# Batch 0's k loaded in two halves, and a GpSimd wait for the second half placed behind the issue of w3's load

## The chip, the cores and the metric

The kernel runs on one core of one Trainium2 chip. The metric is device time in microseconds (us). Three runs of the kernel before took 166.56, 165.96 and 166.01 us; the median is 166.01 us.

The engines are named as the profile names them: PE (TensorE, matrix multiply), PEld (its weight loads), DVE (VectorE), ACT (ScalarE), POOL (GpSimd) and SP (SyncE). Loads and stores run on 16 DMA engines; the queue that issues a load is POOL's (software queue) or SP's (hardware queue).

## The reference, cut to what matters

```python
# q, k, v: (8, 8, 576, 64); phi: (8, 8, 576, 32); w1, w2, w3: (512, 768); w_out: (768, 512)
a = exp(phi - max(phi, axis=2)); a = a / sum(a, axis=2)
k_m = einsum('bhsm,bhsd->bhmd', a, k)
v_m = einsum('bhsm,bhsd->bhmd', a, v)
attn = softmax(q @ k_m.T / 8)          # over the 32 memory slots
x = (attn @ v_m) reshaped to (4608, 512)
h = maximum(maximum(x @ w1, x @ w2), x @ w3)
out = h @ w_out                        # (4608, 512), float32
```

## The kernel before

The kernel holds one batch of the attention at a time, as 4 pairs of heads (`NP`) on 128 partitions. The inputs are float32 in memory; q, k, v and the weights become bfloat16 while they are loaded, which is done by loads issued from GpSimd. phi stays float32; batch 0's phi is loaded in two halves on SP's queue.

No scheduler orders the work. `tc.manual_schedule()` is in force, and the long string in lines 594 to 617 is the program: each word names a step, its index and its batch, and `issue` (L561) emits the instructions of that step on their engines in just this order. Each engine's queue runs in order, so the place of a word fixes its place in every queue that it touches.

The steps that matter here, all of batch 0 unless said otherwise:

- `L1` (`load_kv`, L95) loads all of k, `L3` (`load_q`, L107) all of q, `H1` and `H3` the first and the second half of v by pairs of heads. `H0` and `H2` would do the same for k; the code has them, and the order before doesn't use them.
- `Y2`, `Y3`, `Y0`, `Y1` load w3, w_out, w1 and w2 (L114 and L122).
- `E` (L225) is the exponential of phi on ACT. `B0` (L238) multiplies it with k, and with a column of ones for the sums; its loops run over 9 chunks outside and the 4 pairs of heads inside, so the fifth of its 72 matmuls already reads the second half of k. `N0` and `K0` scale and transpose the result. `I` makes the identity that the transposes use.
- `Q0`, `Q1` (L306) transpose q on DVE, `S` (L320) makes the scores, `M` and `R` the softmax denominators, `X` the normalised attention.
- `W0` to `W2` (L178) transpose w3 on PE, `O0` to `O3` (L189) multiply it with w_out. `D` (L424) folds the weights with v's product: `D0` and `D1` need w1 (and w2), `D2` w2. `F` (L456) is the first layer's matmul and maximum, `T` (L488) the second layer with its output rows.
- `Z` (L155) are matmuls on a tile of zeros, whose result nobody reads.

Of the loads on GpSimd's queue the order is: k, q, (the identity and two small memsets), w3, w_out, v in two halves, w1, w2, then for batch 1 phi, k, q and v, then for batch 2 v, k, phi and q, and so on. The loads share eight completion semaphores in turn, so each issue from the ninth load on waits until the load issued eight before it has landed. Before a buffer is written again, an issue also waits for the engines that still read it.

Of the kernel before, what the change touches and what calls it, by code (L numbers as in the profile page):

```python
# [9 lines left out]
BF16 = mybir.dt.bfloat16  # L10
# [5 lines left out]
def kernel(  # L16
# [12 lines left out]
    nc = tc.nc  # L29

    B, H, S, D = q.shape
    M = phi.shape[-1]
    P = 128
    NP = H // 2
# [10 lines left out]
    const = ctx.enter_context(tc.tile_pool(name="const", bufs=1))  # L45
# [30 lines left out]
    loaded = {}  # L76
# [8 lines left out]
    def load_ph(b):  # L85
        ph = inp.tile([P, NP, NC, M], FP32, name="ph")
        loaded.setdefault(b, {})["ph"] = ph
        dst = ph.rearrange("p j c m -> p j (c m)")
        if b == 0:
            for h in halves:  # L90
                nc.sync.dma_start(out=dst[:, h], in_=by_pair(phi, b)[:, h])
        else:
            nc.gpsimd.dma_start(out=dst, in_=by_pair(phi, b))

    def load_kv(b, i, h=slice(0, NP)):  # L95
        kv = loaded.setdefault(b, {})["kv"] = kvos[b % 2]
        nc.gpsimd.dma_start(  # L97
            out=kv[:, 1 - i, h].rearrange("p j c d -> p j (c d)"),
            in_=by_pair((k, v)[i], b)[:, h],
        )  # L100

    def pack(b, i):
        nc.gpsimd.tensor_copy(  # L103
            out=kvrs[b % 2][:, :, :, D * i : D * (i + 1)], in_=kvos[b % 2][:, 1 - i]
        )

    def load_q(b):  # L107
        qq = inp.tile([P, NP, NC, D], BF16, name="qq")
        loaded.setdefault(b, {})["q"] = qq
        nc.gpsimd.dma_start(  # L110
            out=qq.rearrange("p j c d -> p j (c d)"), in_=by_pair(q, b)
        )

    def load_w(i):  # L114
        w = (moe_w1, moe_w2, moe_w3)[i]
        nc.gpsimd.dma_start(
            out=w_sb[:, :, i], in_=w.rearrange("(j p) f -> p j f", p=P)
        )
# [2 lines left out]

    def load_wo():  # L122
        nc.gpsimd.dma_start(out=wo_sb, in_=moe_w_out.rearrange("(t p) c -> p t c", p=P))  # L123

    load_ph(0)

# [21 lines left out]
    def one_bank():  # L148
        return psum[:, int(next(banks))]
# [5 lines left out]
    def warm_up(n):  # L155

        po = one_bank()
        for _ in range(n):
            nc.tensor.matmul(  # L159
                po[:, 0:BANK], lhsT=warm[:, 0:P], rhs=warm, start=True, stop=True  # L160
            )
# [46 lines left out]
    def w_diff(n):  # L208

        c, end = n * BANK, (n + 1) * BANK  # L210
        while c < end:
            e = min(end, (c // DF + 1) * DF)
            nc.vector.tensor_tensor(
                out=w12[:, :, c:e],
                in0=w12[:, :, c:e],
                in1=w_sb[:, :, 2, c % DF : c % DF + e - c],
                op=ALU.subtract,
            )
            c = e
# [5 lines left out]
    def att_exp(b, js=slice(0, NP)):  # L225
        s = st.setdefault(b, {})
        if "e" not in s:
            s["e"] = work.tile([P, NP, NC, M], BF16, name="e")
        nc.scalar.activation(out=s["e"][:, js], in_=loaded[b]["ph"][:, js], func=AF.Exp)  # L229
# [8 lines left out]
    def att_kv(b, part=None):  # L238
        s = st[b]
        kvp = two_banks()  # L240
        s["kvp", part] = kvp
        kv = loaded[b]["kv"]
        nd = {None: 2 * D + 1, 0: 2 * D, 1: D}[part]
        kvr = kvrs[b % 2]
        for c in range(NC):
            for j in range(NP):
                for a in range(NG):
                    r = slice(HP * a, HP * (a + 1))
                    nc.tensor.matmul(  # L249
                        kvp[M * j : M * (j + 1), a, 0:nd],  # L250
                        lhsT=s["e"][r, j, c, :],
                        rhs={
                            None: lambda: kvr[r, j, c, 0:nd],
                            0: lambda: k_and_ones(kv, r, j, c),
                            1: lambda: kv[r, 0, j, c, :],
                        }[part](),
                        start=(c == 0),
                        stop=(c == NC - 1),
                        tile_position=(HP * a, M * j),
                    )  # L260
# [141 lines left out]
    def att_rec(b, g):  # L402
        s = st[b]
        nc.vector.reciprocal(out=s["sm", g], in_=s["sm", g])  # L404
# [156 lines left out]
    def issue(b, n, swap):  # L561

        i = int(n[1:]) if len(n) > 1 else None
        {
            "I": lambda: [make_identity(nc, ident)]
            + [nc.gpsimd.memset(x[:, :, :, 2 * D : 2 * D + 1], 1.0) for x in kvrs],
            "Y": lambda: load_w(i) if i < 3 else load_wo(),
            "L": lambda: load_ph(b) if i == 0 else load_q(b) if i == 3 else load_kv(b, i - 1),
            "H": lambda: load_kv(b, i % 2, halves[i // 2]),
            "r": lambda: pack(b, i),  # L570
            "E": lambda: [att_exp(b, h) for h in (halves if b == 0 else [slice(0, NP)])],
            "B": lambda: att_kv(b, i),
            "N": lambda: att_kv_norm(b, i),
            "K": lambda: att_kv_t(b, swap, i),
            "Q": lambda: att_q(b, i),
            "S": lambda: att_score(b),
            "a": lambda: att_t(b, i),
            "s": lambda: att_sum(b, i),
            "c": lambda: att_rec(b, i),
            "m": lambda: att_mul(b, i),  # L580
            "X": lambda: (ones_mul if (b, i) in ONES else att_back)(b, i),
            "M": lambda: ones_sum(b, i),
            "R": lambda: ones_rec(b, i),
            "D": lambda: fold(b, i, swap),
            "F": lambda: ffn1(b, i, swap),
            "T": lambda: ffn2(b, i, swap),
            "W": lambda: w3_t(i, swap),
            "O": lambda: w3_o(i, swap),
            "V": lambda: w_diff(i),
            "Z": lambda: warm_up(i),  # L590
        }[n[0]]()


    for w in """
        E@0 L1@0 L3@0 Z25@0 B0@0 I@0 N0@0 Z2@0 K0@0! Q0@0 Q1@0 Z9@0 S@0 Z2@0 M0@0 M1@0
        R0@0 Y2@0 R1@0 W0@0 Y3@0 W1@0 W2@0 Z6@0 O1@0 H3@0 O3@0 O2@0 H1@0 X1@0 B1@0 X0@0 N1@0
        K1@0 O0@0 Y0@0 D1@0! D0@0! D3@0 F8@0 F10@0 F2@0 V0@0 F6@0 F0@0! Y1@0 D2@0 D4@0 F4@0
        L0@1 V1@0 F1@0 E@1 F3@0 L1@1 F5@0 F9@0 F7@0 L3@1 F11@0 B0@1 T3@0 N0@1 K0@1! L2@1 Q1@1
        L2@2 L1@2 Q0@1 L0@2 V2@0 T0@0! L3@2 S@1 T1@0 a0@1 s0@1 c0@1 m0@1 B1@1 N1@1 a1@1 L1@3
        K1@1 s1@1 D0@1 D1@1! D2@1 c1@1 m1@1 X0@1 L3@3 r1@2 X1@1 T2@0! L2@3 F6@1 F10@1 F7@1 F2@1  # L600
        F3@1 F4@1 F0@1 r0@2 E@2 F5@1 F1@1 F11@1 L0@3 L0@4 F8@1 L2@4 F9@1 B@2 D3@1 N@2 Q1@2
        T0@1! K@2 T2@1! r0@3 Q0@2 S@2 a0@2 a1@2 s1@2 c1@2 m1@2 T4@1! D1@2! s0@2 D2@2 c0@2 m0@2
        X1@2 D0@2 T3@1 Q0@3 L3@4 X0@2 Q1@3 T1@1 F0@2 F4@2 F8@2 F6@2 F9@2 E@3 F7@2 r1@3 F5@2
        F10@2 F1@2 B@3 L1@4 D3@2 N@3 L0@5 F2@2 F11@2 E@4 F3@2 L1@5 K@3 r1@4 L2@5 T2@2! S@3 T3@2
        a0@3 s0@3 c0@3 m0@3 D0@3 D2@3 a1@3 s1@3 c1@3 X0@3 D1@3! Q0@4 m1@3 T1@2 L3@5 L2@6 T0@2!
        X1@3 F10@3 r0@4 F2@3 F4@3 E@5 Q1@4 r0@5 F5@3 F3@3 L1@6 F8@3 B@4 N@4 D3@3 F9@3 F6@3
        F11@3 L0@6 K@4 F0@3 F7@3 F1@3 S@4 a0@4 T4@3! s0@4 a1@4 D0@4 c0@4 s1@4 r1@5 c1@4 D3@4
        m0@4 X0@4 Q0@5 T0@3! D1@4! D2@4 B@5 T3@3 m1@4 X1@4 L0@7 F10@4 Q1@5 N@5 F8@4 K@5 F6@4
        F9@4 S@5 F7@4 L3@6 F2@4 F4@4 a0@5 L1@7 a1@5 F0@4 s0@5 r1@6 F3@4 D0@5 r0@6 s1@5 c1@5 E@6
        D3@5 m1@5 c0@5 F1@4 T1@3 L2@7 F11@4 L3@7 E@7 F5@4 m0@5 B@6 D1@5! D2@5 X1@5 N@6 T2@3!  # L610
        X0@5 F6@5 F8@5 Q0@6 Q1@6 K@6 F4@5 F9@5 S@6 F7@5 r0@7 a0@6 F2@5 a1@6 s0@6 c0@6 F0@5
        F10@5 m0@6 F1@5 s1@6 c1@6 F11@5 F5@5 T0@4! F3@5 X0@6 T2@4! r1@7 D0@6 D1@6! Q0@7 B@7
        m1@6 N@7 X1@6 T2@5! K@7 T3@4 Q1@7 S@7 a0@7 F2@6 s0@7 a1@7 s1@7 c1@7 m1@7 c0@7 F4@6
        T4@5! D3@6 D2@7 D0@7! T0@5! D3@7 D2@6 X1@7 m0@7 D1@7! T1@4 X0@7 F6@7 F3@6 T1@5 F4@7
        F8@7 F0@7 F5@6 F10@6 F7@7 F9@7 F10@7 F5@7 F0@6 F11@7 F6@6 F1@7 F7@6 F2@7 F8@6 F11@6
        F9@6 F1@6 F3@7 T0@6! T0@7! T3@5 T2@7! T2@6! T1@6 T1@7 T3@6 T4@7! T3@7
    """.split():
        n, b = w.rstrip("!").split("@")
        issue(int(b), n, w.endswith("!"))
# [30 lines left out]
```

## Time and profile before

| | |
|---|---|
| median of 3 runs | 166.01 us |
| span of the profiled execution, first to last instruction | 163.9 us |
| outside the span, against the median | 2.1 us |
| PE busy | 153.8 us (94%) |
| ACT, DVE, POOL busy | 100.5, 90.4, 68.8 us |
| bytes moved by DMA | 31.77 MB, mean 194 GB/s |
| software queue's share of the 16 engines' time | 68.5% |
| granted TensorE clock, mean | 1.000 |

The page lists one profiled execution. A line of the timeline has a start and a duration in us, an engine, a line of the code, an operation, the tile it writes and the tile it reads, a count, and in square brackets how long the engine sat idle before it and what released it. In the chain of waits, a line is a start, a duration and what the chain ran through: where a DMA stands there, the time is from its issue to its landing. In a table of stages, a row is a stretch of time and gives, per engine, busy time and number of instructions, then the granted clock, the DMA engines' share and what they moved in GB/s. The bytes are counted as they are written, so a load from float32 to bfloat16 counts half of what is read.

The five largest shares of the chain by line are the matmuls of L497 (25%) and L466 (22%), the load of phi (14%), the load of the weights (12%) and the matmuls of L506 (7%).

### The profile page before, as it was taken

Reading aid. Unit: us, or ns where it says so; the run is one execution under the profiler, and the core shown is the slowest. Engines: PE = TensorE matmul, PEld = TensorE weight load, DVE = VectorE, ACT = ScalarE, POOL = GpSimd, SP = SyncE. Lnnn points to the kernel's source line nnn. Section 1 sums busy time; section 2 is a strip of 40 time slices with the busy share of each in tenths; the row PEclk is TensorE's granted clock in tenths of the full one; section 3 lists DMA queues with packets and bytes.
Section 4 is the critical chain, followed back from the end, with each engine's and each line's share of the span. In section 5 each row is a group of like instructions: output and inputs, shape, how many; then the busy total and the mean of one; then the engine's idle time right before and its main releaser. Section 6 shows DMA issues by size and latency. Waiting matters only on the chain.

```text
span 163.9 us, 4837 instructions
## 1 busy us (share of the span) xinstructions
PE 153.8 (94%) x2080; PEld 85.3 (52%) x2080; DVE 90.4 (55%) x181; ACT 100.5 (61%) x151; POOL 68.8 (42%) x70
## 2 busy tenths in 40 slices
PE   7958798999899999999999999999999999999990
PEld 2423544664376436753673565576553467744450
DVE  2013703898837765759399669879749228810000
ACT  4104535935496488778885989994658976323320
POOL 7911115100698276938929986755403200000000
PEclk9999999999999999999999999999999999999999
DMA  5999999999999999999999999996313230014333
GB/s 149 167 201 207 207 209 226 264 208 209 258 310 239 209 272 361 263 219 294 247 265 206 236 352 254 167 235 148 127 72 119 79 128 0 0 68 179 141 128 130
DMA packets 21958, 31.77 MB, mean 194 GB/s; under 512 B 1200, under 2 KB 16560, under 8 KB 21936
## 3 DMA queue, kind: packets, MB, share of 16 engines
q0 software_dynamic: 16064, 21.43, 68.5%
q1 hardware_dynamic: 5728, 9.90, 17.1%
q8 instruction: 16, 0.26, 0.6%
q10 hardware_dynamic: 144, 0.13, 0.2%
q14 instruction: 6, 0.05, 0.1%
HBM read 39.32 MB, written 9.44 MB: 297 GB/s over the span
## 4 chain that ended last, share of the span: by engine, by line
PE 66%; DMA 27%; POOL 3%; issue 1%; ACT 1%; ACTq 0%; POOLq 0%
PE psum L497 25%; PE psum L466 22%; DMA ph<-in_phi_dram 14%; DMA w_sb<-in_moe_w_dram 12%; PE psum L506 7%; PE psum L440 4%; PE psum L249 3%; PE psum L333 2%; PE psum L515 1%; POOL kvo L97 1%; PE psum L538 1%; ACT e L229 1%; PE psum L298 1%; POOL wo_sb L123 1%; POOL qq L110 0%
## 5 line engine op out<-in xcount | busy, mean ns | idle before, releaser
L497 PE MATMUL psum<-wo_sb,hT 128*128 128x512 bf16 x210 | 51.4, 380 | 0.2
L466 PE MATMUL psum<-attn,wp 128*128 128x288 bf16 x384 | 50.5, 286 | 0.1
L479 DVE TENSOR_TENSOR hT<-psum,h 128x576 bf16<-128x576 f32 x48 | 34.2, 749 | 18.2 <-PE psum L466 12.1
L466 PEld LDWEIGHTS <-wp 128*128 128x128 bf16 x384 | 36.7, 98 | 13.2 <-issue 2.0
L172 ACT COPY ot<-psum 128x512 f32<-128x512 f32 x35 | 20.7, 591 | 32.3 <-PE psum L506 25.2
L497 PEld LDWEIGHTS <-hT 128*128 128x128 bf16 x210 | 19.2, 98 | 24.2 <-issue 4.5
L103 POOL COPY kvr<-kvo 128x2304 bf16<-128x2304 bf16 x12 | 25.4, 2116 | 14.1 <-DMA kvo<-in_k_dram 6.4
L172 ACT CAST wp<-psum 128x1024 bf16<-128x1024 f32 (+1 forms) x31 | 29.3, 997 | 3.0 <-PE psum L440 2.1
L170 ACT ACTIVATE h<-psum 128x576 bf16<-128x576 f32 x47 | 28.4, 659 | 3.2 <-PE psum L466 3.1
L409 POOL TENSOR_TENSOR t<-t,sm 128x576 bf16<-128x576 bf16 x14 | 16.1, 1158 | 25.6 <-DVE sm L404 25.5
L506 PE MATMUL psum<-wp,attn 128*128 128x512 bf16 x62 | 18.4, 379 | 0.0
L159 PE MATMUL psum<-warm 128*128 128x512 bf16 x44 | 12.0, 424 | 1.2 <-DVE warm L128 1.2
L313 DVE STREAM_TRANSPOSE qT<-qq 128x576 f32<-128x576 f32 x16 | 11.7, 747 | 1.3 <-DMA qq<-in_q_dram 1.3
L342 ACT ACTIVATE e<-psum 128x576 bf16<-128x576 f32 x16 | 9.6, 652 | 3.7 <-PE psum L333 3.7
L229 ACT ACTIVATE e<-ph 128x1152 bf16<-128x1152 f32 (+1 forms) x9 | 9.6, 1065 | 2.9 <-DMA ph<-in_phi_dram 2.9
L395 DVE TENSOR_REDUCE sm<-t 128x18 f32<-128x576 bf16 x14 | 10.3, 738 | 0.2
L387 DVE STREAM_TRANSPOSE t<-e 128x288 f32<-128x288 f32 x14 | 6.4, 465 | 6.2 <-ACT e L342 6.0
L506 PEld LDWEIGHTS <-attn 128*128 128x128 bf16 x62 | 6.1, 98 | 7.1
L97 POOL DMA_DIRECT2D kvo<-in_v_dram x9 | 6.7, 747 | 7.1 <-PE psum L249 4.1
L249 PEld LDWEIGHTS <-e 64*32 64x32 bf16 x720 | 6.9, 90 | 4.9 <-issue 3.6
L555 DVE COPY ot<-psum 128x256 f32<-128x256 f32 x1 | 0.4, 425 | 15.4 <-PE psum L546 15.4
L110 POOL DMA_DIRECT2D qq<-in_q_dram x8 | 6.2, 769 | 5.9 <-DMA w_sb<-in_moe_w_dram 5.9
(57 smaller groups left out, 113.8 us busy)
## 6 DMA issues: line engine op xcount, KB each, us to landing
out_dram<-ot SPq DMA_DIRECT2D x35, 256.0 KB, 5.6
kvo<-in_k_dram POOLq DMA_DIRECT2D x8, 576.0 KB, 13.3
qq<-in_q_dram POOLq DMA_DIRECT2D x8, 576.0 KB, 12.6
ph<-in_phi_dram POOLq DMA_DIRECT2D x7, 576.0 KB, 15.0
kvo<-in_v_dram POOLq DMA_DIRECT2D x7, 576.0 KB, 16.6
w_sb<-in_moe_w_dram POOLq DMA_DIRECT2D x3, 768.0 KB, 20.3
wo_sb<-in_moe_w_out_dram POOLq DMA_DIRECT2D x1, 768.0 KB, 15.9
ph<-in_phi_dram SPq DMA_DIRECT2D x2, 288.0 KB, 3.1
```

The source lines that it names most:

```text
L103: nc.gpsimd.tensor_copy(out=kvrs[b % 2][:, :, :, D * i : D * (i + 1)], in_=kvos[b % 2][:, 1 - i])
L159: nc.tensor.matmul(po[:, 0:BANK], lhsT=warm[:, 0:P], rhs=warm, start=True, stop=True)
L170: nc.scalar.activation(out=out_, in_=in_, func=AF.Relu)
L172: nc.scalar.copy(out=out_, in_=in_)
L229: nc.scalar.activation(out=s["e"][:, js], in_=loaded[b]["ph"][:, js], func=AF.Exp)
L249: nc.tensor.matmul(kvp[M * j : M * (j + 1), a, 0:nd], lhsT=s["e"][r, j, c, :], rhs={None: lambda: kvr[r, j, c, 0:nd], 0: lambda: k_and_one ...
L313: nc.vector.transpose(out=s["qT"][:, j].rearrange("p j c r e -> p (j c r e)").bitcast(FP32), in_=loaded[b]["q"][:, j].rearrange("p j c d - ...
L409: nc.gpsimd.tensor_tensor(out=t, in0=t, in1=s["sm", g].unsqueeze(2).to_broadcast([P, S // HP, R, 2]), op=ALU.mult,)
L466: nc.tensor.matmul(acc[:, h, 0:SH], lhsT=wps[b][:, g, w * DF + ft * P : w * DF + (ft + 1) * P], rhs=attn[:, g, c0 : c0 + SH], start=(g == ...
L479: nc.vector.tensor_tensor(out=hT[:, ft, (b % 2) * S : (b % 2 + 1) * S].rearrange("p (h n) -> p h n", h=2), in0=a, in1=s["h1", ft], op=ALU.max,
L497: nc.tensor.matmul(po, lhsT=hT[:, fc, c0 : c0 + P], rhs=wo_sb[:, fc, :], start=(n == 0), stop=False,)
L506: nc.tensor.matmul(po, lhsT=attn[:, g, c0 : c0 + P], rhs=wp3s[b][:, g, :], start=False, stop=(g == NG - 1),)
```

## The change

k of batch 0 is loaded by two loads of two pairs of heads each in place of one load of four (`H0 H2` for `L1`). A new step, `G0`, copies two elements of the second half of k (the last pair of heads, one partition) into a new tile `gate` on GpSimd; nobody reads that tile. The copy reads what the second load writes, so GpSimd waits there until it has landed. In the order `G0` stands behind `Y2` and ahead of `Y3`, so on GpSimd's queue it comes after the issue of w3's load and ahead of the issues of w_out, v, w1, w2 and everything behind them. The function has another form, for q, which isn't used.

```diff
+    gate = const.tile([1, 2], BF16, name="gate")
+
+    def wait_for(b, n):
+
+        x = loaded[b]["q"][0:1, 0, 0, 0:2] if n else loaded[b]["kv"][0:1, 1, NP - 1, 0, 0:2]
+        nc.gpsimd.tensor_copy(out=gate, in_=x)
...
+            "G": lambda: wait_for(b, i),
...
-        E@0 L1@0 L3@0 Z25@0 B0@0 I@0 N0@0 Z2@0 K0@0! Q0@0 Q1@0 Z9@0 S@0 Z2@0 M0@0 M1@0
-        R0@0 Y2@0 R1@0 W0@0 Y3@0 W1@0 W2@0 Z6@0 O1@0 H3@0 O3@0 O2@0 H1@0 X1@0 B1@0 X0@0 N1@0
+        E@0 H0@0 H2@0 L3@0 Z25@0 B0@0 I@0 N0@0 Z2@0 K0@0! Q0@0 Q1@0 Z9@0 S@0 Z2@0 M0@0 M1@0
+        R0@0 Y2@0 G0@0 R1@0 W0@0 Y3@0 W1@0 W2@0 Z6@0 O1@0 H3@0 O3@0 O2@0 H1@0 X1@0 B1@0 X0@0 N1@0
```

## The prediction

> **What bounds the kernel now.** I read the chain of waits first, to see what the end hangs on, then the two queues around the change.
>
> ```profile
> 6.53 20.26 DMA w_sb<-in_moe_w_dram
> 26.79 0.59 issue
> 27.39 23.77 DMA ph<-in_phi_dram
> 51.17 1.17 ACT e L229
> 52.39 0.81 PE psum L249 x70
> ```
>
> From 6.5 to 51.2 us the chain is two loads, each some 20 us from issue to landing; from there it is PE without a break. A load of 768 KB that takes 20 us was queued, not slow. The trace's packet records show the queue: packets of 1536 bytes (w3) begin at 9.96 us, as the first engines end q, and packets of 1024 bytes (w_out) at 13.9, as they end w3. Each of the 16 DMA engines works through the loads in the order of issue, without a pause.
>
> GpSimd's queue, timeline:
>
> ```profile
> 1.24 0.93 POOL L97 DMA_DIRECT2D kvo<-in_k_dram  x1 [0.80 <-POOLq L634]
> 2.17 0.75 POOL L110 DMA_DIRECT2D qq<-in_q_dram  x1
> ...
> 3.57 0.76 POOL L116 DMA_DIRECT2D w_sb<-in_moe_w_dram  x1
> 4.33 0.83 POOL L123 DMA_DIRECT2D wo_sb<-in_moe_w_out_dram  x1
> 5.14 1.42 POOL L97 DMA_DIRECT2D kvo<-in_v_dram  x2
> 6.53 1.53 POOL L116 DMA_DIRECT2D w_sb<-in_moe_w_dram  x2
> 10.09 0.76 POOL L93 DMA_DIRECT2D ph<-in_phi_dram  x1 [2.03 <-DMA kvo<-in_k_dram]
> ```
>
> Eight loads are issued by 8.06 us, long before the engines reach most of them; the next issue waits for k.
>
> PE's queue, timeline:
>
> ```profile
> 9.94 0.80 PE L249 MATMUL psum<-kvo,e 64*32 64x128 bf16 x72 [1.54 <-DMA kvo<-in_k_dram]
> ...
> 20.25 4.04 PE L192 MATMUL psum<-wo_sb,w3T 128*128 128x512 bf16 x18 [0.97 <-DMA wo_sb<-in_moe_w_out_dram]
> ...
> 30.65 0.30 PE L440 MATMUL psum<-w_sb,kvt 64*32 64x256 bf16 x8
> ```
>
> PE goes at the pace of the loads: it waits 1.54 us for k, 0.97 for w_out, and its weight load waits 0.2 for w2 at 30.65. A load counts as landed when the last of 16 engines has written its completion. By the records, 14 of k's 16 completions come between 6.88 and 8.01 us, median 7.50, and the last two at 8.72 and 9.53. These engines stay late: the last completion is at 12.37 for q, 16.12 for w3, 19.92 for w_out, 26.54 for w1 and 30.28 for w2, each time 1.5 us after the thirteenth. So PE and the 51 us of the load chain hang on one engine that fell behind before 9.6 us.
>
> The stages show when the engines are slow (last number: GB/s):
>
> ```profile
> 4.00:5.00 1.00, 1.00 (x4) 0.35 (x3) 0.00 (x0) 0.51 (x2) 1.00 (x2) 1.00 0.94 129
> 5.00:6.00 1.00, 1.00 (x6) 0.49 (x5) 0.00 (x0) 0.37 (x1) 1.00 (x3) 1.00 1.06 160
> 6.00:7.00 1.00, 1.00 (x7) 0.45 (x5) 0.00 (x0) 0.00 (x0) 1.00 (x2) 1.00 1.20 189
> 7.00:8.00 1.00, 1.00 (x6) 0.43 (x5) 0.00 (x0) 0.00 (x0) 1.00 (x2) 1.00 1.13 174
> 8.00:9.00 1.00, 0.40 (x2) 0.00 (x0) 0.00 (x0) 0.00 (x0) 0.06 (x1) 1.00 1.21 202
> 9.00:10.00 1.00, 0.06 (x9) 0.09 (x17) 0.00 (x0) 0.00 (x0) 0.00 (x0) 1.00 1.17 189
> 10.00:11.00 1.00, 1.00 (x74) 0.71 (x73) 0.17 (x2) 0.00 (x0) 0.76 (x1) 1.00 1.19 201
> 11.00:12.00 1.00, 0.61 (x5) 0.23 (x4) 0.61 (x2) 0.01 (x1) 0.00 (x0) 1.00 1.16 210
> ```
>
> The steady rate is 208 to 210. Short of 208 the stages lose 0.38, 0.23, 0.09, 0.16, 0.03, 0.09 and 0.03 us: 1.0 us for the mean engine, nothing later. The late engine loses its 1.0 plus the 2.0 by which 9.53 lies behind the median: about 3 times the mean. The poor stretch covers the burst of issues (1.24 to 8.06) plus about 2 us, and k's own first packet comes 2.3 us after its issue begins.
>
> **The split of k.** One more issue: v's two halves cost 1.42 us together, so 0.7 each. k's second half is issued by 2.9 us, q by 3.65, w3 by 5.1, each 0.7 later than now. A load is ready for the engines 1.34 us after its issue ends (k: 3.51 less 2.17). The second half is then ready at 4.2 with the first busy until about 5.5; q at 5.0, needed at 6.9; w3 at 6.4, needed at 10.0. All covered, by 1.3, 1.9 and 3.6 us; without cover each would cost its 0.7. The identity ends at about 4.2 and is used at 11.66. One more completion per engine costs 0.02 us (its record is 22 ns). PE can run 4 of 72 matmuls (0.04 us) before the second half: nothing.
>
> **The wait.** Behind it on GpSimd's queue stand w_out, v twice, w1, w2, batch 1's phi and k. An issue that waits for a load starts 0.56 us after it (10.09 against 9.53). The copy isn't in the trace: between 0.10 (memset of one column) and 2.12 us (copy of 2304 columns). I take 0.1, as it moves two elements. With k no earlier than now, w_out is issued from 10.2 to 11.0 and ready at 12.4; the first engine wants it at 13.9. Cover 1.5 us; a copy of 2.12 would overrun it by 0.5. Then v to 12.5, w1 and w2 to 14.0, phi to 14.8, k to 15.5. Their packets are wanted from 17.7 (v), 20.5 (w1) and 24.3 (w2) on. Batch 1's q waits for w3 to land (16.12), as now. From there the queue is the old one.
>
> **What it buys.** Issues stop between 5.1 and about 10 us while k and q transfer. If the slow packets follow the issues, the losses after 6 us (0.40 of 1.0 for the mean engine) go away there, times 3 for the late engine: 1.2 us. Bounds: nothing, if they do not follow the issues, and 1.8, if all from 5.1 on goes (0.61 times 3). The six issues then come as a burst at 10.2 to 14.8. The nearest row is the burst of three at 25.31 to 28.14: by the records its packets of 28 to 31 us ran over their usual time by 0.03 us per engine in all. Twice that, times 3, is 0.2 given back; the other bound is 1.2, the whole again. Sum: 1.2 less 0.2 less 0.02, so 1.0 us earlier at k, q, w3, w_out, w1, w2 and, at 51.17, batch 2's phi. PE follows one for one, since w3's transposes, w_out's product and the folds are each released by these landings. The span goes from 163.9 to 162.9; with the 2.1 us that the median has outside the span, 165.0 us.
>
> The Trainium skill speaks against this. "DMA: Bandwidth & Descriptors", section "Latency and other measured facts", says that two DMA engines, 7 and 15, usually lag, and guesses at the ports of the partitions that hold the software queue's descriptor rings, which all engines read. The trace agrees on two that lag most (8.72 and 9.53); it doesn't show their numbers. By reading alone, though, the lag would grow with every load, and the gain would be nothing: 166.0 us. Here it stands still after 10 us, from 12.37 against a median of 10.66 (q) to 26.54 against 24.82 (w1): 1.71 and 1.72.
>
> **Rivals.**
> *No net effect, 166.0 us (165.2 to 166.8).* The engines are slow because they start, whatever GpSimd does; or the lag leaves k and comes back on w_out. For it: the worst loss, 0.61 of 1.0, lies before 6 us, under issues that the change keeps, and single later issues (13.00, 16.71) cost no visible rate. Against it: slowness lasts to 10 us, with q's packets slow to 10.1 and those after it at their usual time.
> *Slower, 166.9 us: the burst collects the lag again, in the weights.* The start keeps 60% of the 2.0 us lag, 1.2; six back-to-back issues at the start's price (2.0 over 8, 0.25 each) add 1.5: 2.7, so 0.7 more than now, plus 0.2 for the mean rate. Place: between 12 and 17 us, on w3 and w_out. It decides when w_out's last completion comes after 19.92. For it: 6 issues follow without a gap, as at the start. Against it: the burst at 25 us cost a tenth of that per issue.
> *Slower: the issues come too late.* Read as drawn, the chain has 20.26 us from w1 and w2's issue to landing, and 6 us later issue would end at 172. Against it: the time is queueing. With the long copy it would be 0.5, so 166.5.
> *The change doesn't do what it says:* the wait holds nothing back that matters, as in the first rival.
>
> **How the numbers follow.** Forecast 0.46, no net effect 0.29, burst 0.21, late issues 0.04. Faster by over 0.5% (0.83 us, about what a measurement of this kernel can tell from no change) is the forecast's case: 0.46; same 0.29; slower 0.25. The forecast's own range is 164.2 to 165.2 (gain 1.8 down to 0.8). The whole, with the slower cases, is 164.2 to 167.1.
>
> **What would show it.** Right: k's last landing near 8.5 and PE's first matmul on it near 8.9; w_out's product near 19.2; the fold of w2 near 29.6; phi of batch 2 near 50.2; GB/s above 190 from 6 to 10 us and near 208 from 12 to 17. Wrong: k earlier but w_out's product still at 20.25 (the lag moved); a dip in GB/s at 12 to 17 (burst); a DMA share below 0.9 near 13 to 14 (starved); or PE, though released earlier, waiting for something else by 52 us.

## The result, and the profile after

| | before | after |
|---|---|---|
| median of 7 runs | 166.01 us (165.55 to 166.73) | 164.87 us (164.30 to 165.42) |
| ratio, with 95% interval | | 0.9925 (0.990 to 0.995) |
| span of the profiled execution | 163.9 us | 163.7 us |

The kernel became 0.75% faster, 1.14 us on the medians. The two profiled executions differ by only 0.2 us. The profiled execution of the changed kernel, the first of its series, was the slowest of seven: 165.42 us with a span of 163.7, where the other six had spans of 162.5 to 163.5. Which execution of the kernel before was profiled isn't on record, but of 35 later runs of it, with spans of 163.6 to 165.4, a span of 163.9 is among the shortest. So the two traces show less than the change is worth, and the verdicts below rest on the timed runs; the traces say where things moved in one execution.

GpSimd's queue in the changed kernel, timeline (start, duration, engine, line, operation, tiles, count, and in brackets the idle time before):

```profile
1.24 1.60 POOL L97 DMA_DIRECT2D kvo<-in_k_dram  x2 [0.80 <-POOLq L642]
2.84 0.77 POOL L110 DMA_DIRECT2D qq<-in_q_dram  x1
...
4.26 0.76 POOL L116 DMA_DIRECT2D w_sb<-in_moe_w_dram  x1
9.27 0.17 POOL L130 COPY gate<-kvo 1x2 bf16<-1x2 bf16 x1 [4.25 <-DMA kvo<-in_k_dram]
9.39 0.82 POOL L123 DMA_DIRECT2D wo_sb<-in_moe_w_out_dram  x1
10.21 1.43 POOL L97 DMA_DIRECT2D kvo<-in_v_dram  x2
11.61 1.54 POOL L116 DMA_DIRECT2D w_sb<-in_moe_w_dram  x2
13.10 0.80 POOL L93 DMA_DIRECT2D ph<-in_phi_dram  x1
```

The wait is there, 4.25 us long, and the copy takes 0.17 us. The issues behind it start at 9.39, a little ahead of the 10.2 that was worked out for a k as late as before.

PE's queue of the changed kernel, timeline:

```profile
9.16 0.86 PE L256 MATMUL psum<-kvo,e 64*32 64x128 bf16 x72
...
20.09 4.04 PE L199 MATMUL psum<-wo_sb,w3T 128*128 128x512 bf16 x18 [1.06 <-DMA wo_sb<-in_moe_w_out_dram]
...
30.49 0.30 PE L447 MATMUL psum<-w_sb,kvt 64*32 64x256 bf16 x8
```

k's matmul comes 0.78 us earlier than before (9.94) and no longer waits for k: it starts as PE's 25 matmuls on zeros end. The product with w_out and the fold of w2 come only 0.16 us earlier (20.25 and 30.65). By the prediction's own signs, which put that product near 19.2, this trace speaks for a lag that moved from k to later loads. The stages of the changed kernel show a place where time is lost (last number: GB/s):

```profile
6.00:7.00 1.00, 1.00 (x6) 0.39 (x5) 0.00 (x0) 0.00 (x0) 0.00 (x0) 1.00 1.13 183
7.00:8.00 1.00, 1.00 (x7) 0.41 (x6) 0.00 (x0) 0.00 (x0) 0.00 (x0) 1.00 1.17 186
8.00:9.00 1.00, 1.00 (x6) 0.38 (x4) 0.00 (x0) 0.00 (x0) 0.00 (x0) 1.00 1.17 196
9.00:10.00 1.00, 1.00 (x74) 0.77 (x74) 0.00 (x0) 0.00 (x0) 0.73 (x2) 1.00 1.20 206
...
14.00:15.00 1.00, 0.78 (x12) 0.36 (x5) 0.00 (x0) 0.88 (x2) 0.64 (x1) 1.00 1.16 182
15.00:16.00 1.00, 0.63 (x4) 0.14 (x2) 0.00 (x0) 0.97 (x3) 0.00 (x0) 1.00 1.19 193
16.00:17.00 1.00, 0.77 (x14) 0.78 (x15) 0.04 (x1) 0.97 (x2) 0.54 (x1) 1.00 1.25 181
17.00:18.00 1.00, 0.95 (x15) 0.78 (x14) 1.00 (x2) 0.97 (x2) 0.21 (x1) 1.00 1.19 192
```

At 9 to 10 us the engines move 206 GB/s, against 189 before. At 14 to 18 us there is a dip to 181 to 193, which the kernel before doesn't have (205 to 208). By the records of completions, k's last one came at 8.93 us instead of 9.53, and w_out's last one at 19.73 instead of 19.92: 0.60 us gained, 0.41 given back. Both numbers compare two single executions; in a second trace of the kernel before (below), w_out's product comes at 20.67.

The chain of waits is again made of loads up to 51 us, now with the wait for k in it. w1 and w2 now take 15.00 us from issue to landing instead of 20.26, and land no later: what was cut is time in the queue.

### The profile page after: what moved, and what is told of

It reads as the page before. It is cut to its first block, busy times and chain, and to the rows that moved or that the text cites. A ratio compares the mean times of both kernels' runs of the same rounds, so it can differ in the third digit from the quotient of the medians.

```text
span 163.7 us, 4819 instructions
## 1 busy us (share of the span) xinstructions
PE 153.0 (93%) x2060; PEld 85.5 (52%) x2080; DVE 90.4 (55%) x181; ACT 100.5 (61%) x151; POOL 69.7 (43%) x72
## 4 chain that ended last, share of the span: by engine, by line
PE 65%; DMA 28%; POOL 2%; issue 2%; ACT 1%; POOLq 0%; ACTq 0%
PE psum L504 25%; PE psum L473 22%; DMA ph<-in_phi_dram 15%; DMA w_sb<-in_moe_w_dram 9%; PE psum L513 7%; DMA kvo<-in_k_dram 4%; PE psum L447 4%; PE psum L256 3%; PE psum L340 1%; POOL kvo L97 1%; PE psum L522 1%; PE psum L545 1%; ACT e L236 1%; PE psum L305 1%; POOL wo_sb L123 0%
## 5 line engine op out<-in xcount | busy, mean ns | idle before, releaser
L504 PE MATMUL psum<-wo_sb,hT 128*128 128x512 bf16 x193 | 49.7, 380 | 1.4 <-issue 0.6
L504 PEld LDWEIGHTS <-hT 128*128 128x128 bf16 x210 | 19.2, 98 | 24.1 <-issue 4.3
L166 PEld LDWEIGHTS <-warm 128*128 128x128 bf16 x44 | 4.6, 111 | 7.4 <-issue 3.5
```

The source lines that it names most:

```text
L166: nc.tensor.matmul(po[:, 0:BANK], lhsT=warm[:, 0:P], rhs=warm, start=True, stop=True)
L504: nc.tensor.matmul(po, lhsT=hT[:, fc, c0 : c0 + P], rhs=wo_sb[:, fc, :], start=(n == 0), stop=False,)
```

## The experiments

Up to here the time fits the prediction's story. The first question was which half of the change makes the gain. The second was whether the traces of one execution can be trusted, so the kernel before was run once more.

**The kernel before, again.** No edit.

> The kernel before once more, for the spread from one execution to the next of the late engine. Theory (the slow packets follow GpSimd's burst of issues): k's matmul again starts at 9.6 to 10.4 us, w_out's product 10 to 10.5 us behind it, ratio 1.00. Rival (the lag is an accident of the first profiled execution): k's matmul starts anywhere from 8.5, and the lag between the median and the last of k's completions, 2.0 us there, is below 1 us here.

Measured: ratio 1.002 (0.999 to 1.005), k's matmul at 10.30 us, w_out's product at 20.67. k's last three completions came at 9.38, 9.74 and 9.82 us against a median of 7.9. The late engines are no accident of the first trace. This execution lost more at the start (stages from 4 to 8 us at 103, 138, 164 and 150 GB/s), and ended at the same time.

**The split alone.** The change without its wait.

```diff
-        R0@0 Y2@0 G0@0 R1@0 W0@0 Y3@0
+        R0@0 Y2@0 R1@0 W0@0 Y3@0
```

> k in two halves, no wait. Theory: the split buys nothing, ratio 0.998 to 1.002 (165.7 to 166.3 us), k's matmul at 9.6 to 10.4 us, six to eight issues back to back as before. Rival (the split is what helps, since k's first half is ready earlier and PE's first matmuls need only that): ratio 0.990 to 0.995, k's matmul near 9.2.

Measured: 164.93 us, ratio 0.9928 (0.990 to 0.995). This is the whole gain, without any wait. The theory's 0.998 to 1.002 was wrong, and the rival's ratio right. The rival's reason isn't seen: in the trace all 72 matmuls run in one piece from 9.03 us, behind PE's own matmuls on zeros, when both halves of k had landed (6.93 and 8.48).

**The wait alone.** k in one load, with the wait behind w3's issue.

```diff
-        E@0 H0@0 H2@0 L3@0
+        E@0 L1@0 L3@0
```

> k in one load, with the wait. Theory: all of the gain, ratio 0.991 to 0.994 (164.5 to 165.0 us), k's matmul at 8.6 to 9.2 us, w3's transposes at 15.5 to 16.2. Rival (the split is what helps): 0.998 to 1.002.

Measured: 166.22 us, ratio 1.001 (0.999 to 1.004): nothing. PE's queue in this kernel, timeline:

```profile
10.52 0.80 PE L256 MATMUL psum<-kvo,e 64*32 64x128 bf16 x72 [0.90 <-DMA kvo<-in_k_dram]
```

Its stages (last number: GB/s):

```profile
6.00:7.00 1.00, 1.00 (x4) 0.31 (x3) 0.00 (x0) 0.00 (x0) 0.00 (x0) 1.00 1.18 164
7.00:8.00 1.00, 1.00 (x6) 0.44 (x5) 0.00 (x0) 0.00 (x0) 0.00 (x0) 1.00 1.01 144
8.00:9.00 1.00, 1.00 (x6) 0.44 (x5) 0.00 (x0) 0.00 (x0) 0.00 (x0) 1.00 1.16 188
9.00:10.00 1.00, 0.62 (x3) 0.10 (x1) 0.00 (x0) 0.00 (x0) 0.00 (x0) 1.00 1.16 191
```

GpSimd issued nothing between 4.33 and 10.57 us here, and yet the engines were slow to 10 us, and k's matmul was the latest of all. The split alone, with GpSimd issuing up to 8.8 us, is no slower over the same stages:

```profile
6.00:7.00 1.00, 1.00 (x7) 0.40 (x5) 0.00 (x0) 0.00 (x0) 1.00 (x2) 1.00 1.04 144
7.00:8.00 1.00, 1.00 (x6) 0.49 (x5) 0.00 (x0) 0.00 (x0) 1.00 (x3) 1.00 1.14 180
8.00:9.00 1.00, 1.00 (x6) 0.29 (x3) 0.00 (x0) 0.00 (x0) 0.78 (x2) 1.00 1.20 194
9.00:10.00 1.00, 1.00 (x75) 0.78 (x74) 0.11 (x1) 0.00 (x0) 0.76 (x1) 1.00 1.20 204
```

So the slow packets at the start don't follow GpSimd's issues.

**The split, with a pause that waits for nothing.** Two memsets on buffers that are written again later stand where the copy stood.

```diff
-        x = loaded[b]["q"][0:1, 0, 0, 0:2] if n else loaded[b]["kv"][0:1, 1, NP - 1, 0, 0:2]
-        nc.gpsimd.tensor_copy(out=gate, in_=x)
+        for x in kvrs:
+            nc.gpsimd.memset(x[:, :, :, 0:D], 0.0)
```

> k in two halves; in place of the copy that waits for k, two memsets of 2304 columns on buffers that are written later, so that GpSimd is busy for 4 to 5 us and waits for no load. Theory (it is the pause in the issues that counts, not k's landing): ratio 0.991 to 0.995, GB/s from 6 to 9 us at 185 to 200, as with the wait, and the dip at 14 to 18 us as with the wait. Rival (the wait itself matters, its place tied to k): no gain, 0.998 to 1.002.

Measured: ratio 0.994 (0.991 to 0.997), w_out issued at 8.94 us, a dip to 195 GB/s at 14 to 16 us. The ratio is as the theory said, but the split alone gives it too, so this run says nothing for the pause.

Why does the split help? Four more runs asked for the load's place in the queue, the semaphores, PE's idle time, and the dip.

**A small load ahead of k.** The kernel before with 128 rows of 64 elements of k read first into a tile of its own.

```diff
+    first = const.tile([P, D], BF16, name="first")
+    nc.gpsimd.dma_start(out=first, in_=k[0, 0, 0:P, :])
```

> The kernel before (k in one load, no wait) with a small load of 128 rows of 64 elements of k into a tile of its own ahead of it, so that there are nine early loads and k isn't the first. A (k's own split is what evens out its late engine): ratio 0.997 to 1.004, k's matmul at 9.8 to 10.6 us. B (the first load of the queue bears the slow start, or the completion semaphores shifted by one are what helps): ratio 0.990 to 0.996, k's matmul at 8.7 to 9.3.

Measured: ratio 0.995 (0.992 to 0.998), k's matmul at 8.86, k's last completion at 8.44 us. k itself is still one load, and most of the gain is there. This speaks for B.

**q in two halves, k whole.**

```diff
+        for h in halves if b == 0 else [slice(0, NP)]:
+            nc.gpsimd.dma_start(
+                out=qq[:, h].rearrange("p j c d -> p j (c d)"), in_=by_pair(q, b)[:, h]
```

> k in one load, q of batch 0 in two. A: ratio 0.996 to 1.002, k's matmul still at 9.8 to 10.5 us. B by the semaphores (nine loads before the tenth, as in the change): 0.990 to 0.996. C (PE's idle time ahead of k's matmul and the clock that falls after it): 1.000, since k is as late as before.

Measured: ratio 1.002 (1.000 to 1.004). Nine early loads, and with them the shift of the completion semaphores, aren't it. The traced execution had k's matmul at 8.98 and w_out's product at 19.59, both as early as in the kernels that gain, which the timed runs don't bear out: k's last completion came at 8.5 us in that trace, and the kernel is no faster. One execution's landings can mislead.

**More matmuls on zeros ahead of k.**

```diff
-        E@0 L1@0 L3@0 Z25@0 B0@0
+        E@0 L1@0 L3@0 Z31@0 B0@0
```

> The kernel before with 31 in place of 25 matmuls on zeros, which carry PE to about 11.0 us, past k's landing. C (what the split saves is PE's idle time of 1.5 to 2 us ahead of k, after which the granted clock can fall to half for 3.4 us): ratio 0.990 to 0.995, mean clock at 0.995 or more in all runs. A: 0.998 to 1.003, since w3 and w_out land as late as before, with at most 0.2 us from the clock.

Measured: ratio 1.010 (1.007 to 1.013), slower, which neither side expected. Up to 82 us it goes as the kernel before went (within 0.4 us); then PE stands still, in a place of dense small matmuls:

```profile
86.70 0.47 PE L333 MATMUL psum<-qT,kvt 32*32 32x288 bf16 x30
88.19 0.30 PE L333 MATMUL psum<-qT,kvt 32*32 32x288 bf16 x2 [1.02 <-issue]
```

Two matmuls of a group of 32 come 1.02 us late and wait for nothing that the profile shows; in the kernel before the group runs through. Six added matmuls far earlier moved all of PE's later instructions on by twelve. That it is the fetching of instructions is a guess, which the traces don't settle: a load of 16 KB on the instruction queue starts at 85.79 us here, and at 85.64 in the kernel before, which doesn't stall. The question on C stayed open.

**The same number of matmuls on zeros, moved.**

```diff
-        Z25@0 B0@0 I@0 N0@0 Z2@0 K0@0! Q0@0 Q1@0 Z9@0 S@0
+        Z31@0 B0@0 I@0 N0@0 Z2@0 K0@0! Q0@0 Q1@0 Z5@0 S@0
...
-        W1@0 W2@0 Z6@0 O1@0
+        W1@0 W2@0 Z4@0 O1@0
```

> The kernel before with six of the matmuls on zeros moved: 31 ahead of k's matmul in place of 25, 5 in place of 9 after it, 4 in place of 6 ahead of w_out's product, so that PE's instruction count ahead of the 87 us at which six more cost 1.0 us is as before. C (PE's idle time ahead of k and the half clock after it are part of what the split saves): ratio 0.994 to 0.998, mean clocks of 0.995 or more. A late engine alone: 0.999 to 1.002.

Measured: ratio 1.001 (0.998 to 1.004), k's matmul at 10.28 us, as the matmuls on zeros end. One of 12 runs had a mean clock below 0.992, against 12 of the 35 runs of the kernel before beside it. PE's idle time ahead of k, and the clock, are not where the gain comes from. In this run's trace the group of dense small matmuls, at 86.39 us, runs through again.

**The change with four more waits**, so that the issues come in pairs. `G1` to `G4` make the same small copy from q, w3, w_out and v.

```diff
-        Z6@0 O1@0 H3@0
+        Z6@0 O1@0 G1@0 H3@0
...
-        O0@0 Y0@0
+        O0@0 G2@0 Y0@0
...
-        L0@1 V1@0
+        G3@0 L0@1 V1@0
...
-        F7@0 L3@1
+        F7@0 G4@0 L3@1
```

> The change with four more such waits, so that the issues come in pairs: w_out behind k, v behind q, w1 and w2 behind w3, batch 1's phi and k behind w_out, its q and v behind v. Burst theory (issues in a burst slow the packets 2 to 5 us later, seen at 14 to 18 us in the changed kernel): no dip there, GB/s 203 or more from 12 to 20, w_out's product 0.3 to 0.5 us earlier than 20.09, ratio 0.988 to 0.991. If the issues do not matter: 0.992 to 0.994, as with the split alone.

Measured: ratio 0.996 (0.994 to 0.999), 203 to 213 GB/s from 12 to 20 us. The dip of 14 to 18 us is gone, as the burst theory said, but the burst isn't shown to be its cause. Four other kernels of this section have neither a wait nor a burst, and yet have the dip in their traces: those with 128 rows of k or of w2 read first, with q in halves and with the matmuls moved run at 152 to 199 GB/s from 14 to 18 us. Two stages of the one with w2's rows:

```profile
14.00:15.00 1.00, 0.72 (x10) 0.30 (x5) 0.00 (x0) 0.88 (x2) 0.00 (x0) 1.00 1.07 152
15.00:16.00 1.00, 0.64 (x4) 0.14 (x2) 0.00 (x0) 0.97 (x3) 0.00 (x0) 1.00 1.19 184
```

The wait alone has the burst, and only one slow stage (191 GB/s at 14 to 15). What the six traces with the dip share is that w_out's first packets came early, at 13.50 to 13.89 us; in the other eight they came at 13.88 to 14.36, and latest of all in this run. So the dip's cause stays open. The time is no better than with the split alone: w_out's product came at 20.08, and the fold of w2 at 31.01.

Two runs asked whether the first load's size counts, one whether its source does.

**k in loads of one and of three pairs of heads**, no wait (`H0` takes one, `H2` three, in place of `L1`).

```diff
-            "H": lambda: load_kv(b, i % 2, halves[i // 2]),
+            "H": lambda: load_kv(
+                b, i % 2, (halves if i % 2 else [slice(0, 1), slice(1, NP)])[i // 2]
+            ),
```

> k in two loads, of one and of three pairs of heads, no wait. If a short first load is what evens out the engines: ratio 0.990 to 0.995, as with halves, k's last completion at 8.2 to 9.0 us. If what counts is that k's end is a load of its own: 0.995 to 1.000, k's last completion after 9.3.

Measured: ratio 0.995 (0.993 to 0.998), k's last completion at 8.61 us.

**k in loads of three and of one pair**: the same edit with `slice(0, 3)` and `slice(3, NP)`.

> k in two loads, of three and of one pair of heads, no wait. If a short first load is what counts: most of the gain is gone, ratio 0.996 to 1.001, k's last completion at 9.2 to 10.0 us. If any split counts, or the number of loads: 0.990 to 0.995 as with halves.

Measured: ratio 1.001 (0.998 to 1.004), last completions at 9.95 and 10.10 us. A split isn't enough; the first load has to be short, a quarter or a half of k and not three quarters.

**The small first load, from w2 instead of k.**

```diff
-    nc.gpsimd.dma_start(out=first, in_=k[0, 0, 0:P, :])
+    nc.gpsimd.dma_start(out=first, in_=moe_w2[0:P, 0:D])
```

> As the small first load that took 128 rows of k, but taken from w2. If the queue's first load bears a slow start, whatever it reads: ratio 0.992 to 0.998 as with k's rows (0.995). If k's memory has to be touched once: 0.999 to 1.003, k's matmul at 9.8 to 10.5 us.

Measured: ratio 1.001 (0.998 to 1.004), k's matmul at 9.66 us. A small first load of another tensor does nothing that the timed runs show; the interval just touches that of k's rows (0.992 to 0.998). So it is not the queue's first load as such: by the timed runs, what helps is that a short load of k's own rows goes ahead of the rest of k. The trace doesn't show that difference. k's last completion came at 8.80 us, as early as in the kernels that gain, and the matmul came late because PE was still at its 25 matmuls on zeros:

```profile
1.19 8.53 PE L162 MATMUL psum<-warm 128*128 128x512 bf16 x25 [1.19 <-DVE warm L131]
9.66 0.80 PE L252 MATMUL psum<-kvo,e 64*32 64x128 bf16 x72
```

All runs side by side:

| kernel | first load of k | pause in the issues | ratio (95%) | k's matmul, traced | k's last completion, traced |
|---|---|---|---|---|---|
| before, again | whole | no | 1.002 (0.999 to 1.005) | 10.30 us | 9.82 us |
| the change | half | yes | 0.9925 (0.990 to 0.995) | 9.16 | 8.93 |
| split alone | half | no | 0.9928 (0.990 to 0.995) | 9.03 | 8.48 |
| split and pause | half | yes | 0.994 (0.991 to 0.997) | 8.73 | 8.31 |
| four more waits | half | yes, spread | 0.996 (0.994 to 0.999) | 8.50 for 4, 9.04 for 68 | 8.74 |
| one pair, three pairs | quarter | no | 0.995 (0.993 to 0.998) | 8.02 for 2, 8.94 for 70 | 8.61 |
| 128 rows of k ahead | 128 rows | no | 0.995 (0.992 to 0.998) | 8.86 | 8.44 |
| three pairs, one pair | three quarters | no | 1.001 (0.998 to 1.004) | 9.85 for 6, 10.45 for 66 | 10.10 |
| wait alone | whole | yes | 1.001 (0.999 to 1.004) | 10.52 | 10.10 |
| 128 rows of w2 ahead | whole | no | 1.001 (0.998 to 1.004) | 9.66 | 8.80 |
| q in halves | whole | no | 1.002 (1.000 to 1.004) | 8.98 | 8.5 |
| matmuls moved | whole | no | 1.001 (0.998 to 1.004) | 10.28 | 9.45 |
| six matmuls more | whole | no | 1.010 (1.007 to 1.013) | 10.21 | 9.80 |

The column of the first load sorts the ratios and the column of the pause doesn't. The last column sorts them with two exceptions: w2's rows ahead and q in halves have an early k and no gain.

## Why the prediction was right in its number and wrong in its cause

**What bounds the kernel: right in the traces.** k, w3, w_out, w1 and w2 land in the order of issue, and PE follows the last completion of w_out: its product started 0.33 us after it before and 0.36 us after it in the changed kernel, and in the two kernels 0.19 and 0.16 us earlier agree. One reading was off: w2's last completion (30.28) came 0.8 us after its thirteenth and not 1.5. The late engines appear in six of the eight traces in which k's first load is long: k's last completions are at 9.53 and 9.82 us in the two traces of the kernel before, at 10.10 with the wait alone and with three pairs first, and at 9.80 and 9.45 with the matmuls added and moved. The traces with q in halves (8.5) and with w2's rows ahead (8.80) are the exceptions. Where the first load of k is short, all six traces have them at 8.31 to 8.93.

**The split costs its issues under cover: right, and the step "nothing" failed.** Its two issues took 1.60 us, q and w3 moved 0.7 us later, and nothing starved. But the step gave the split no effect, and the split is the whole effect: 0.9928 alone.

**The wait's cover: right.** The copy took 0.17 us (0.1 assumed), and w_out's first packets moved at 13.76 us, no later than before (13.88).

**What it buys: this step failed.** It said that issues stop while k and q transfer, that the slow packets follow the issues, and so that the 0.40 us lost after 6 us go away, three times over for the late engine. The wait alone stops the issues for 6 us and changes neither the rate (164, 144, 188, 191 GB/s) nor k's landing nor the time. Nor does the change lower the loss itself: short of 208, the stages from 4 to 10 us lose 0.99 and 1.54 us in the two traces of the kernel before, 1.22 with the wait alone, 1.19 with the split alone and 1.09 with both. What differs in the traces with a short first load is how the loss is spread: k's last completion lies 0.6 to 1.2 us behind its median, against 1.9 to 2.6 in the six traces with late engines. w_out's product then starts at 19.59 to 20.13 us, against 20.25 to 20.98. That this is what shortens the timed runs is argued and not shown: the two exceptions have the small lag (1.5 and 1.3 us) and the early product (19.59 and 19.86) in their traces, and no gain in their timed runs.

The 0.2 given back by the burst isn't settled. The dip at 14 to 18 us costs the mean engine 0.39 us in the changed kernel's trace (the four stages short of 207 GB/s), where 0.07 was assumed, and k's gain of 0.60 us shrank to 0.19 at w_out. But kernels without a burst have the dip too, and in the run without it the time was no better.

**The sum, 1.0 us against 1.14 measured, agrees by luck, as far as these runs show.** Its main term, 1.2 us, was to come from the stopped issues, which are worth nothing; the split was put at nothing and is worth the whole. Nor do the traces place 1.14 us anywhere: they differ by 0.16 us at w_out's product and by 0.2 in the span. The 2.1 us outside the span was also off: each run of the changed kernel lies 1.7 to 1.9 us over its own span (165.42 against 163.7), and so do the 35 later runs of the kernel before, so the profiled execution there wasn't the median one.

**The rivals.** "No net effect" is what the wait alone does, and its reason, that the engines are slow because they start, whatever GpSimd does, fits the stages of all traces. For the burst there is the dip at the place named, but the dip doesn't need a burst, and the timed runs came out faster and not slower. The row that spoke against the forecast stood in the prediction: 0.61 of the 1.0 us lay before 6 us. What it lacked was a rival in which the split has an effect of its own.

The Trainium skill ("DMA: Bandwidth & Descriptors", section "Latency and other measured facts") says that two engines usually lag. The traces of the kernel before agree, with two or three late (8.72 and 9.53 us; 9.38, 9.74 and 9.82).

**What stays open.** Why a short first load of k's rows makes the kernel faster, when one of w2's rows doesn't, isn't settled. A cost of first reaching k's memory, paid while little is queued behind it, would fit the timed runs, but no run shows it, and the one trace with w2's rows has k as early as with k's own. What makes the dip at 14 to 18 us is open as well. Nor is it shown why the first execution of a series, the one that is traced, gives less of the gain than the later ones.

## What to carry to other kernels

Where a change has two parts, price each part alone before looking for the mechanism of the whole: here the part that looked like bookkeeping was all of it, and the split alone, without the wait and its tile, is the simpler kernel at the same time. Where loads are queued in order, look at the last completion of the first load and not at its mean: in the first trace here the lag at q's last completion was still there at w1's, and a short first piece of the same tensor is a cheap thing to try. A single traced execution can't confirm an effect of half a per cent; take its landings as a hint and the intervals of timed runs as the verdict.

## What the runs showed of the hardware that was not expected

The start-up loss is there in every trace, some 0.7 to 1.7 us per engine between 4 and 10 us against 208 GB/s, with single packets of 1152 bytes that took up to 1.55 us instead of 0.107; from 11 us on nearly all packets take their usual time, but for the dip at 14 to 18 us that six of the 14 traces have.

PE's granted clock can fall to half for 3.4 us after PE has waited for k. In the second trace of the kernel before it is seen in the stages (the third number from the right is the granted clock):

```profile
10.00:12.00 2.00, 1.33 (x74) 0.80 (x74) 0.78 (x3) 0.00 (x0) 0.76 (x1) 0.94 1.19 209
12.00:14.00 2.00, 1.98 (x7) 0.88 (x8) 0.95 (x2) 0.37 (x1) 0.69 (x1) 0.50 1.16 210
14.00:16.00 2.00, 2.00 (x38) 0.66 (x36) 0.48 (x1) 0.00 (x0) 0.05 (x1) 0.70 1.20 207
```

15 of 35 runs of the kernel before had a mean clock of 0.991 or less, and none of the 43 runs of the change, the split alone, the split with the pause and one and three pairs; with four more waits it was one of 12. The runs of the kernel before with the lower clock were 0.3 us slower in the median (166.46 against 166.13 us), so this is a small part at most, and keeping PE busy there gained nothing.

Twelve more instructions early in PE's queue cost 1.02 us at 88 us, where PE waited for nothing that the profile shows; with six matmuls on zeros fewer after them (the matmuls moved), the stall is gone.
